# Turning the token tiles of five experts by VectorE in 32 by 32 blocks instead of by TensorE

## The chip, the cores and the metric

The kernel runs on one core of a Trainium2 chip. The metric is device time in microseconds (us). Before the change it is 337.43 us, the median of 3 runs from 336.81 to 337.83. A kernel drives five engines, each with its own queue in program order: TensorE (PE, matmuls and transposes; its weight loads are PEld), VectorE (DVE), ScalarE (ACT), GpSimd (POOL) and SyncE (SP). DMAs are issued from a queue of one of them and then run on 16 DMA engines.

## The reference

The program is an attention followed by a mixture of experts whose routing is a hash of the token's id. Cut to what matters:

```
q_n, k_n = rmsnorm(q, g_q), rmsnorm(k, g_k)          # 8 batches, 12 heads, 448 x 64
attn = softmax(q_n @ k_n^T / sqrt(64)) ; x = attn @ v  # as 3584 tokens x 768
expert = token_ids * 2654435761 % 8
for e in 0..7:
    xe = x[expert == e]                               # some 450 tokens
    out[expert == e] = max(xe @ w1[e], 0) @ w2[e]     # 768 x 1024, 1024 x 768
```

## The kernel before, in words

The first part (to about 160 us) is the attention. It writes x as 16-bit floats to a scratch tensor in HBM. The change does not touch it. The second part goes through the experts 0 to 7, one after the other; the stage of an expert is its two products.

Each expert has room for 480 tokens, in four row tiles: three of 128 tokens (kt 0 to 2) and one of 96 (kt 3). For each row tile, GpSimd issues an indirect DMA (`gather`, L230) that collects 128 rows of x from the scratch tensor into SBUF, tokens on the partitions. The tiles of two experts stand in a ring of eight places in the tile `kr` (`xg_ring`): the four places of expert e are used again by expert e+2. In the stage of expert e, `fetch(e + 2, ...)` (L1262) issues the four gathers of expert e+2.

The first product (`gemm1`, L1002) needs the tokens along the free dimension, so a row tile has to be turned: `turn` (L1055) calls `put_xT` (L238), which makes six TensorE transposes of 128 by 128 (L242) into a PSUM bank and one copy by VectorE (L244) into the tile `xT`. There are two buffers of xT. For the experts 2 to 6 these turns stand in front of the four column steps of the second product of the expert before (`before[e, kt]`, L1241 and L1272). The tiles of expert 1 are turned in the stage of expert 0, and those of expert 7 by four DMA transposes on SP's queue (L1065).

`gemm1` makes 48 matmuls of 480 columns: eight blocks of 128 rows of h, six matmuls each, in three PSUM buffers. After each block a ReLU brings it to `h_sb`, by ScalarE for the even blocks (L1011) and by VectorE for the odd ones (L1013). `gemm2` (L1018) goes over four column steps; each makes 16 matmuls (L1024) into one of two PSUM buffers `o_ps`, a copy to SBUF (`o_sb`, five buffers, L1034; ScalarE for steps 0 and 2, VectorE for 1 and 3), and an indirect DMA on GpSimd's queue that scatters the rows to the output (L1037).

Weights are loaded by GpSimd's queue too (L1090), three pieces of w1 and two of w2 an expert, converted from 32 to 16 bits on the way. The pieces of expert e+3 are issued in the stage of expert e, in the same queue as the scatters and the gathers. A DMA of this queue waits for the one eight places before it, since they share a semaphore. The order of the work is written out by hand: engines take their instructions in the order of the code.

Of the kernel before, what the change touches and what calls it, by code (L numbers as in the profile page):

```python
# [10 lines left out]
FP16 = mybir.dt.float16  # L11
# [9 lines left out]
def kernel(  # L21
# [12 lines left out]
    nc = tc.nc  # L34
# [3 lines left out]
    E = moe_w1.shape[0]  # L38
    F = moe_w1.shape[2]
    P = 128  # L40
    HP = H // 2
    CO = DIN // P
# [7 lines left out]
    CAP = 512  # L50
    FIT = 480
    LAST = FIT - 3 * P
    KT = CAP // P
# [31 lines left out]
    xg_ring = k_keep[:].rearrange("p (r d) -> p r d", d=DIN)  # L85
# [152 lines left out]
    def put_xT(xg, xT, col, bank, copy=None):  # L238
        xT_ps = bank.rearrange("p (c t) -> p c t", c=CO)
        n = LAST if col == KT - 1 else P  # L240
        for co in range(CO):
            nc.tensor.transpose(xT_ps[:, co, 0:n], xg[0:n, co * P:(co + 1) * P], ident16[0:n, 0:n])  # L242
        dst = xT[:, col] if xT is xT_e else xT[:, :, col * P:(col + 1) * P]
        (copy or nc.vector.tensor_copy)(dst[:, :, 0:n], xT_ps[:, :, 0:n])  # L244
# [719 lines left out]
    with tc.manual_schedule(), \  # L964
# [10 lines left out]
        def w1_view(e, w1_sb):  # L975
            return w1_sb[:].rearrange("p c (o f) -> p c o f" if e == 0 else "p c (f o) -> p c o f",
                                      o=FO)
# [13 lines left out]
        def gemm1(w1v, xT, h_sb, c0, c1, both=True, after=(), apart=0):  # L991
            banks = {}

            def products(fo, a0, a1):
                if fo not in banks:
                    banks[fo] = ps_h.tile([P, 512], FP32, name="h_ps")
                dst = banks[fo][:, a0 - c0:a1 - c0]
                if xT is xT_e:
                    dst = dst.rearrange("p (k t) -> p k t", t=P)
                for co in range(CO):  # L1000
                    src = xT[:, a0 // P:a1 // P, co, :] if xT is xT_e else xT[:, co, a0:a1]
                    nc.tensor.matmul(dst, lhsT=w1v[:, co, fo, :], rhs=src,  # L1002
                                     start=(co == 0), stop=(co == CO - 1))

            for fo in range(apart):
                products(fo, c0, c1 - P)
            for fo in range(FO):
                products(fo, c1 - P if fo < apart else c0, c1)
                h_ps = banks.pop(fo)
                if fo % 2 == 0 or not both:  # L1010
                    nc.scalar.activation(h_sb[:, fo, c0:c1], h_ps[:, :c1 - c0], AF.Relu)  # L1011
                else:
                    nc.vector.tensor_scalar(out=h_sb[:, fo, c0:c1], in0=h_ps[:, :c1 - c0],  # L1013
                                            scalar1=0.0, scalar2=None, op0=ALU.max)
                for f in after[fo] if after else ():
                    f()

        def gemm2(w2_sb, h_sb, col, idx, free=True, between=None, last=False):  # L1018
            w = LAST if free and col == KT - 1 else P
            o_ps = [ps_o.tile([P, DIN], FP32, name="o_ps")]  # L1020
            o_ps.append(ps_o.tile([P, DIN], FP32, name="o_ps") if last else o_ps[0])
            for d0, d1 in ((0, 512), (512, DIN)):
                for fo in range(FO):
                    nc.tensor.matmul(o_ps[d0 > 0][0:w, d0:d1], lhsT=h_sb[:, fo, col * P:col * P + w],  # L1024
                                     rhs=w2_sb[:, fo, d0:d1],
                                     start=(fo == 0), stop=(fo == FO - 1))
                if between and d0 == 0:
                    between()
                if last and d0 == 0:
                    o_sb = m_o.tile([P, DIN], FP32, name="o_sb")  # L1030
                    nc.scalar.copy(o_sb[0:w, 0:512], o_ps[0][0:w, 0:512])
            if not last:
                o_sb = m_o.tile([P, DIN], FP32, name="o_sb")
                (nc.vector.tensor_copy if col % 2 else nc.scalar.copy)(o_sb[0:w], o_ps[0][0:w])  # L1034
            else:
                nc.scalar.copy(o_sb[0:w, 512:DIN], o_ps[1][0:w, 512:DIN])
            scat = nc.gpsimd.indirect_dma_start(  # L1037
                out=out[:, :], out_offset=bass.IndirectOffsetOnAxis(ap=idx[0:w], axis=0),
                in_=o_sb[0:w], in_offset=None, bounds_check=N - 1, oob_is_err=False)
            if free:  # L1040

                tc.declare_no_dep(scat.ins, group="scatters", reason="disjoint rows")
                tc.add_to_no_dep_group("scatters", scat.ins)

        xgs = {c: xg_ring[:, c] for c in range(KT, 2 * KT - 1)}
        xTs = {0: xT_e}
# [8 lines left out]
        def turn(e, kt, copy=None):  # L1055
            if e not in xTs:
                xTs[e] = m_x.tile([P, CO, CAP], FP16, name="xT")
            bank = ps_x.tile([P, DIN], FP16, name="xT_ps")
            put_xT(xgs.pop(e * KT + kt), xTs[e], kt, bank[:], copy)

        def turn_by_dma(e):
            xTs[e] = m_x.tile([P, CO, CAP], FP16, name="xT")
# [173 lines left out]
        t = lambda e, kt: (lambda: turn(e, kt))  # L1236
        t0 = lambda e, kt: (lambda: turn(e, kt, nc.scalar.copy))
        before, between = {}, {}
        for e in range(1, E - 2):
            for kt in range(KT):  # L1240
                before[e, kt] = [t(e + 1, kt)]  # L1241
        before[0, 0], before[0, 1] = [t0(1, 0)], [t0(0, KT - 1)]
        between[0, 1] = t0(1, 1)
        before[0, 2] = [lambda: gemm1_late(w1_view(0, w_tiles[0][0]), xTs.pop(0), hs[0], EARLY, FIT)]
# [7 lines left out]
        for e in range(E):  # L1252
            w1_sb, w2_sb = w_tiles[e]
            h_sb = hs[e] = m_h.tile([P, FO, CAP], FP16, name="h_sb")
            after = [plan.get((e, "g", fo), []) for fo in range(FO)]
            if e == 0:
                gemm1(w1_view(e, w1_sb), xTs[e], h_sb, 0, EARLY, False, after, 2)
            else:
                if e == E - 2:
                    turn_by_dma(E - 1)  # L1260
                if e < E - 2:
                    fetch(e + 2, range(KT))  # L1262
                gemm1(w1_view(e, w1_sb), xTs.pop(e), h_sb, 0, FIT, True, after)
            if e:
                w_next(2)
            if e == 2:
                n_ov = nc.values_load(novi[0:1, 0:1], min_val=0, max_val=NOV)
            if e == E - 1:
                nc.gpsimd.drain()
            for kt in range(KT):  # L1270
                c = e * KT + kt
                for f in before.get((e, kt), []):  # L1272
                    f()
                gemm2(w2_sb, h_sb, kt, gidx[:, c:c + 1], between=between.get((e, kt)),
                      last=(c == E * KT - 1))
                for f in plan.get((e, "k", kt), []):
                    f()
                if e or kt > 1:
                    w_next(1)
            w_next(len(queue))  # L1280
            if e + 4 < E:
                queue += w_pieces(e + 4)
# [47 lines left out]
```

## Time and profile before

| what | value |
|---|---|
| median of 3 runs | 337.43 us (336.81 to 337.83) |
| the profiled execution | 337.81 us, span of the core 336.3 us |
| PE, DVE, ACT, POOL busy | 324.1, 197.6, 188.1, 149.4 us |
| first matmul of gemm1 of experts 1 to 7 | 182.80, 204.18, 225.57, 246.95, 268.34, 289.72, 309.84 us |
[...]

PE is busy for 96% of the span. The stages of experts 1 to 5, in which the next expert's tiles are turned by TensorE, take 21.38 us each; that of expert 6 takes 20.12 us. In the stages of experts 2 to 5 the DMA engines have no free time (a share over 1 means that packets overlap).

### The profile page before, as it was taken

To read this page: it belongs to the slowest core of one execution; us is meant where nothing else is said; L and a number is where in the kernel's file an instruction comes from. 1 tells how busy PE (TensorE), PEld (TensorE's weight loads), DVE (VectorE), ACT (ScalarE), POOL (GpSimd) and SP (SyncE) were. 2 spreads that over 40 slices of the span, in tenths; PEclk is the share of its full clock that TensorE was granted. 3 is DMA by queue.
4 is the path that set the end of the run, shared out by engine and by line. 5 is a ranking of instruction groups with operands and counts; after the bars stand their busy time and mean duration, and the time that the engine had idled before them with its cause. 6 is when DMAs were issued, how large, how long until landed. Compare 5 with 4: busy or idle time off the path is not lost. (4 is left out here: it accounts for less than half of the span.)

```text
span 336.3 us, 9185 instructions
## 1 busy us (share of the span) xinstructions
PE 324.1 (96%) x3885; PEld 226.0 (67%) x3885; DVE 197.6 (59%) x427; ACT 188.1 (56%) x287; POOL 149.4 (44%) x207
## 2 busy tenths in 40 slices
PE   7799999999999999998999999999999999999992
PEld 3567777777777776666677767677676676766751
DVE  4699999998989899984793343232323223222210
ACT  4699999999999999998443212202022021211211
POOL 8799925324340100003665853637557374303122
PEclk9999999999999999999999999999999999999998
DMA  6999999999999999332587899999999999923013
GB/s 132 201 201 204 211 231 197 242 200 237 203 244 211 248 225 238 69 84 72 154 167 215 167 209 246 263 274 250 258 263 255 271 244 255 281 47 133 25 51 117
DMA packets 45602, 65.54 MB, mean 195 GB/s; under 512 B 12727, under 2 KB 33423, under 8 KB 45432
## 3 DMA queue, kind: packets, MB, share of 16 engines
q0 software_dynamic: 39072, 58.32, 85.8%
q1 hardware_dynamic: 6328, 6.50, 7.2%
q8 instruction: 31, 0.51, 0.6%
q10 hardware_dynamic: 160, 0.11, 0.1%
q14 instruction: 11, 0.09, 0.1%
HBM read 89.29 MB, written 17.30 MB: 317 GB/s over the span
## 5 line engine op out<-in xcount | busy, mean ns | idle before, releaser
L660 ACT ACTIVATE expT<-sc_ps 128x896 bf16<-128x896 f32 x144 | 125.0, 959 | 2.5 <-PE sc_ps L637 2.2
L1024 PEld LDWEIGHTS <-h_sb 128*128 128x128 f16 (+1 forms) x512 | 51.2, 104 | 30.3 <-ACT h_sb L1011 0.4
L1024 PE MATMUL o_ps<-w_sb,h_sb 128*128 128x512 f16 (+3 forms) x384 | 66.3, 326 | 0.0
L1037 POOL DMA_INDIRECT out_dram<-o_sb,gidx x32 | 35.0, 1095 | 62.4 <-ACT o_sb L1034 29.6
L1011 ACT ACTIVATE h_sb<-h_ps 128x480 f16<-128x480 f32 (+1 forms) x36 | 19.9, 553 | 68.4 <-PE h_ps L1002 64.4
L230 POOL DMA_INDIRECT kr<-x_scratch,gidx x32 | 32.7, 1021 | 50.6 <-DVE qT L629 36.6
L1002 PEld LDWEIGHTS <-w_sb 128*128 128x128 f16 x300 | 39.7, 135 | 16.0 <-issue 0.3
L1002 PE MATMUL h_ps<-xT,w_sb 128*128 128x480 f16 x240 | 49.4, 366 | 0.0
L1013 DVE TENSOR_SCALAR h_sb<-h_ps 128x480 f16<-128x480 f32 x28 | 18.4, 658 | 47.2 <-PE h_ps L1002 42.2
L1034 ACT COPY o_sb<-o_ps 128x768 f32<-128x768 f32 x16 | 12.8, 799 | 59.3 <-PE o_ps L1024 47.0
L637 PE MATMUL sc_ps<-qT,kT 64*128 64x448 f16 x288 | 44.3, 356 | 0.8 <-DVE qT L629 0.4
L678 PEld LDWEIGHTS <-expT 128*128 128x128 bf16 x846 | 36.8, 97 | 9.5 <-DVE x_sb L738 4.6
L678 PE MATMUL av_ps<-v,expT 128*128 128x65 bf16 x828 | 41.5, 193 | 0.3 <-DVE x_sb L738 0.2
L1034 DVE COPY o_sb<-o_ps 128x768 f32<-128x768 f32 (+1 forms) x15 | 14.3, 956 | 37.6 <-PE o_ps L1024 32.9
L306 POOL DMA_DIRECT2D vr<-in_v_dram x36 | 23.8, 673 | 18.3 <-DMA kr<-in_k_dram 10.4
L738 DVE TENSOR_TENSOR x_sb<-av_ps,srec 128x448 f16<-128x448 f32 x47 | 29.3, 623 | 1.3
L663 ACT ACTIVATE expT<-sc_ps 128x448 bf16<-128x448 f32 x48 | 28.6, 598 | 0.1
L387 PEld LDWEIGHTS <-ident 128*128 128x128 f16 x576 | 22.7, 97 | 7.9 <-issue 2.8
L683 PE MATMUL av_ps<-v,expT 128*128 128x130 bf16 x138 | 24.0, 220 | 0.0
L1024 PE MATMUL o_ps<-kr,h_sb 128*128 128x512 f16 (+3 forms) x128 | 21.6, 326 | 0.0
L244 DVE COPY xT<-xT_ps 128x768 f16<-128x768 f16 (+1 forms) x21 | 11.0, 524 | 17.9 <-PE xT_ps L242 15.8
L1002 PE MATMUL h_ps<-xT,qr 128*128 128x480 f16 x96 | 19.8, 366 | 0.0
(225 smaller groups left out, 441.8 us busy)
## 6 DMA issues: line engine op xcount, KB each, us to landing
w_sb<-in_moe_w_dram POOLq DMA_DIRECT2D x18, 512.0 KB
w_sb<-in_moe_w_dram POOLq DMA_DIRECT2D x8, 768.0 KB
kr<-in_k_dram POOLq DMA_DIRECT2D x7, 672.0 KB
qr<-in_q_dram POOLq DMA_DIRECT2D x7, 672.0 KB
x_scratch<-x_sb SPq DMA_DIRECT2D x15, 288.0 KB, 6.9
w_sb<-in_moe_w_dram POOLq DMA_DIRECT2D x2, 1536.0 KB
qr<-in_moe_w_dram POOLq DMA_DIRECT2D x6, 512.0 KB
vr<-in_v_dram POOLq DMA_DIRECT2D x14, 192.0 KB
```

The costliest lines, as they stand in the source:

```text
L230: nc.gpsimd.indirect_dma_start(out=xg[0:idx.shape[0], :], out_offset=None, in_=x_dram[0:rows, :], in_offset=bass.IndirectOffsetOnAxis(ap=i ...
L306: eng.dma_start(out=dst[64 * half:64 * half + 64, :, s0:s0 + cnt, :].rearrange("p n s d -> p n (s d)"), in_=runs(t, h0 + HP * hh, 1, n, to ...
L637: nc.tensor.matmul(sc[:, hh, :S], lhsT=kT[64 * hh:64 * hh + 64, P * j:P * j + P], rhs=qT[64 * hh:64 * hh + 64, :], start=True, stop=True)
L660: nc.scalar.activation(expT[:, 2 * j:2 * j + 2, :], sc[:, :, :S], AF.Exp, bias=0.0, scale=1.0)
L663: nc.scalar.activation(expT[:, 6, :], sc[:, 0, :S], AF.Exp, bias=0.0, scale=1.0)
L678: nc.tensor.matmul(av[:, 2 * t + hh, :], lhsT=expT[:, tl(hh, j), P * t:P * t + P], rhs=v8[:, i, vs(hh, j), 0:D + 1], start=(hh == 0 and t ...
L683: nc.tensor.matmul(av[:, 2 * t:2 * t + 2, :], lhsT=expT[:, 6, P * t:P * t + P], rhs=v8[:, i, 0::7, 0:D + 1], start=False, stop=False)
L738: nc.vector.tensor_tensor(out=xs[b][:, :, hp * D:hp * D + D], in0=av[:, :, :D], in1=srec[:, :, None].to_broadcast([P, SL, D]), op=ALU.mult)
L1002: nc.tensor.matmul(dst, lhsT=w1v[:, co, fo, :], rhs=src, start=(co == 0), stop=(co == CO - 1))
L1024: nc.tensor.matmul(o_ps[d0 > 0][0:w, d0:d1], lhsT=h_sb[:, fo, col * P:col * P + w], rhs=w2_sb[:, fo, d0:d1], start=(fo == 0), stop=(fo == ...
L1034: (nc.vector.tensor_copy if col % 2 else nc.scalar.copy)(o_sb[0:w], o_ps[0][0:w])
L1037: scat = nc.gpsimd.indirect_dma_start(out=out[:, :], out_offset=bass.IndirectOffsetOnAxis(ap=idx[0:w], axis=0), in_=o_sb[0:w], in_offset=N ...
```

## The change

A new function `turn_blocks(e)` turns the four row tiles of an expert with 16 VectorE instructions, SBUF to SBUF. Each of them takes 32 partitions (32 tokens of each of the four tiles) and writes 32 other partitions; within an instruction each block of 32 by 32 is turned. 12 of them handle four tiles, 4 of them (the last 32 tokens) three tiles, since the fourth has 96 tokens. It is called for the experts 2 to 6, at the start of the stage of the expert before, behind the gathers of the expert after. The 24 TensorE transposes and four VectorE copies for each of these experts go. In the stages of experts 1 to 5 all eight ReLUs and all four output copies are ScalarE's; in the stages of experts 0, 6 and 7 they are shared as before.

```
--- before.py
+++ after.py
@@ -1015,7 +1015,7 @@
                 for f in after[fo] if after else ():
                     f()
 
-        def gemm2(w2_sb, h_sb, col, idx, free=True, between=None, last=False):
+        def gemm2(w2_sb, h_sb, col, idx, free=True, between=None, last=False, by_v=True):
             w = LAST if free and col == KT - 1 else P
             o_ps = [ps_o.tile([P, DIN], FP32, name="o_ps")]
             o_ps.append(ps_o.tile([P, DIN], FP32, name="o_ps") if last else o_ps[0])
@@ -1031,7 +1031,7 @@
                     nc.scalar.copy(o_sb[0:w, 0:512], o_ps[0][0:w, 0:512])
             if not last:
                 o_sb = m_o.tile([P, DIN], FP32, name="o_sb")
-                (nc.vector.tensor_copy if col % 2 else nc.scalar.copy)(o_sb[0:w], o_ps[0][0:w])
+                (nc.vector.tensor_copy if by_v and col % 2 else nc.scalar.copy)(o_sb[0:w], o_ps[0][0:w])
             else:
                 nc.scalar.copy(o_sb[0:w, 512:DIN], o_ps[1][0:w, 512:DIN])
             scat = nc.gpsimd.indirect_dma_start(
@@ -1057,6 +1057,21 @@
                 xTs[e] = m_x.tile([P, CO, CAP], FP16, name="xT")
             bank = ps_x.tile([P, DIN], FP16, name="xT_ps")
             put_xT(xgs.pop(e * KT + kt), xTs[e], kt, bank[:], copy)
+
+        def turn_blocks(e):
+            xT = xTs[e] = m_x.tile([P, CO, CAP], FP16, name="xT")
+            c0 = e * KT % (2 * KT)
+            xg = xg_ring[:, c0:c0 + KT].rearrange("p k (c m r) -> p k m c r", m=4, r=32)
+            dst = xT[:].rearrange("p c (g r) -> p c g r", r=32)
+            for kt in range(KT):
+                xgs.pop(e * KT + kt)
+            for i in range(4):
+                n = KT if 32 * i < LAST else KT - 1
+                g = slice(i, i + 4 * (n - 1) + 1, 4)
+                for m in range(4):
+                    nc.vector.transpose(
+                        out=dst[32 * m:32 * m + 32, :, g].rearrange("p c k r -> p k c r"),
+                        in_=xg[32 * i:32 * i + 32, 0:n, m])
 
         def turn_by_dma(e):
             xTs[e] = m_x.tile([P, CO, CAP], FP16, name="xT")
@@ -1236,9 +1251,6 @@
         t = lambda e, kt: (lambda: turn(e, kt))
         t0 = lambda e, kt: (lambda: turn(e, kt, nc.scalar.copy))
         before, between = {}, {}
-        for e in range(1, E - 2):
-            for kt in range(KT):
-                before[e, kt] = [t(e + 1, kt)]
         before[0, 0], before[0, 1] = [t0(1, 0)], [t0(0, KT - 1)]
         between[0, 1] = t0(1, 1)
         before[0, 2] = [lambda: gemm1_late(w1_view(0, w_tiles[0][0]), xTs.pop(0), hs[0], EARLY, FIT)]
@@ -1260,7 +1272,8 @@
                     turn_by_dma(E - 1)
                 if e < E - 2:
                     fetch(e + 2, range(KT))
-                gemm1(w1_view(e, w1_sb), xTs.pop(e), h_sb, 0, FIT, True, after)
+                    turn_blocks(e + 1)
+                gemm1(w1_view(e, w1_sb), xTs.pop(e), h_sb, 0, FIT, e >= E - 2, after)
             if e:
                 w_next(2)
             if e == 2:
@@ -1272,7 +1285,7 @@
                 for f in before.get((e, kt), []):
                     f()
                 gemm2(w2_sb, h_sb, kt, gidx[:, c:c + 1], between=between.get((e, kt)),
-                      last=(c == E * KT - 1))
+                      last=(c == E * KT - 1), by_v=e in (0, E - 2, E - 1))
                 for f in plan.get((e, "k", kt), []):
                     f()
                 if e or kt > 1:
```

On VectorE, this is what stands before in the stage of one expert of 2 to 5: four ReLUs (`h_sb<-h_ps`), four copies of turned tiles and two output copies.

```order
L1013 TENSOR_SCALAR h_sb<-h_ps 128x480 x4
L244 COPY xT<-xT_ps 128x6x128 x2
L1034 COPY o_sb<-o_ps 128x768
L244 COPY xT<-xT_ps 128x6x128
L244 COPY xT<-xT_ps 128x6x96
L1034 COPY o_sb<-o_ps 96x768
```

And this is what stands there now, in the stages of expert 2 and, from the last row on, of expert 3 (`kr_69` holds the ring of gathered tiles; the names in brackets are the semaphores waited for, DMASW those of GpSimd's DMAs).

```order
L1072 STREAM_TRANSPOSE xT<-kr_69 32x4x6x32 [waits DMASW5_49,DMASW6_49,DMASW0_49,DMASW7_49,PE_49,Activation_49]
L1072 STREAM_TRANSPOSE xT<-kr_69 32x4x6x32 x11
L1072 STREAM_TRANSPOSE xT<-kr_69 32x3x6x32 x4
L1280 TENSOR_LOAD novi [waits DVE_49]
L1072 STREAM_TRANSPOSE xT<-kr_69 32x4x6x32 [waits DMASW4_49,DMASW3_49,DMASW5_49,DMASW2_49,PE_49]
```

VectorE's stage now holds nothing but the 16 transposes, and the first of them waits for all four gathers of the expert to be turned.

On ScalarE, before, for the stages of experts 1 and 2 and the start of 3 (`h_sb` is a ReLU, `o_sb` an output copy):

```order
L1011 ACTIVATE h_sb<-h_ps 128x480 x4
L1034 COPY o_sb<-o_ps 128x768 x2
L1011 ACTIVATE h_sb<-h_ps 128x480 x4
L1267 TENSOR_LOAD novi
L1034 COPY o_sb<-o_ps 128x768 x2
```

And now, for the same stages:

```order
L1011 ACTIVATE h_sb<-h_ps 128x480 x8
L1034 COPY o_sb<-o_ps 128x768 x3
L1034 COPY o_sb<-o_ps 96x768
L1011 ACTIVATE h_sb<-h_ps 128x480 x8
L1280 TENSOR_LOAD novi
```

ScalarE has eight ReLUs and four copies in a stage where it had four and two. On TensorE the 24 weight loads and transposes of L242 are gone from each of the five stages, and on GpSimd the order is unchanged, but the first gather of an expert now waits for VectorE where it waited for TensorE.

## Rows read from the trace of the kernel before

**Rows 1.** Windows by stage: length, busy us (instructions) of PE, PEld, DVE, ACT, POOL, PEclk, DMA, GB/s.

```profile
182.80:204.18 21.38, 21.38 (x138) 14.68 (x137) 7.42 (x13) 3.88 (x6) 13.00 (x16) 1.00 0.91 186
204.18:225.57 21.39, 21.39 (x139) 14.70 (x138) 6.56 (x10) 3.88 (x6) 11.56 (x13) 1.00 1.06 262
...
268.34:289.72 21.38, 21.38 (x138) 14.69 (x137) 6.49 (x10) 3.88 (x6) 12.51 (x14) 1.00 1.03 266
289.72:309.84 20.12, 20.12 (x114) 13.44 (x113) 4.54 (x6) 3.88 (x6) 3.89 (x4) 1.00 0.47 109
```

**Rows 2.** Timeline of TensorE, experts 2 and 6: start, us, engine, line.

```profile
204.18 9.88 PE L1002 MATMUL h_ps<-xT,qr 128*128 128x480 f16 x48
213.90 0.50 PE L242 MATMUL xT_ps<-ident,kr 128*128 128x128 f16 x6
214.24 2.76 PE L1024 MATMUL o_ps<-kr,h_sb 128*128 128x512 f16 x16
...
289.72 9.88 PE L1002 MATMUL h_ps<-xT,qr 128*128 128x480 f16 x48
299.44 10.56 PE L1024 MATMUL o_ps<-kr,h_sb 128*128 128x512 f16 x64
```

**Rows 3.** Timeline of GpSimd: start, us, engine, line [idle before it, and its releaser].

```profile
185.74 0.96 POOL L230 DMA_INDIRECT kr<-x_scratch,gidx  x1 [0.30 <-issue]
...
191.73 1.08 POOL L230 DMA_INDIRECT kr<-x_scratch,gidx  x1 [0.30 <-issue]
...
208.64 1.07 POOL L1037 DMA_INDIRECT out_dram<-o_sb,gidx  x1 [0.50 <-DMA kr<-x_scratch,gidx]
...
211.60 0.58 POOL L1090 DMA_DIRECT2D w_sb<-in_moe_w_dram  x1
...
227.43 1.08 POOL L1037 DMA_INDIRECT out_dram<-o_sb,gidx  x1 [3.42 <-DMA w_sb<-in_moe_w_dram]
...
234.99 1.08 POOL L230 DMA_INDIRECT kr<-x_scratch,gidx  x1 [0.62 <-issue]
...
247.65 1.07 POOL L1037 DMA_INDIRECT out_dram<-o_sb,gidx  x1 [3.42 <-DMA w_sb<-in_moe_w_dram]
...
267.80 1.07 POOL L1037 DMA_INDIRECT out_dram<-o_sb,gidx  x1 [3.46 <-DMA kr<-in_moe_w_dram]
...
279.86 0.98 POOL L230 DMA_INDIRECT kr<-x_scratch,gidx  x1 [0.34 <-issue]
```

**Rows 4.** Timeline of SP's queue: the transposes of expert 7's tiles.

```profile
288.92 6.88 SPq L1065 DMA_TRANSPOSE xT<-kr  x4
```

**Rows 5.** DMAs that write the tile xT: the time from issue to landing.

```profile
DMA to landing us min/median/max: 2.8/4.3/4.8
```

**Rows 6.** Windows (as Rows 1) around the gathers of expert 2.

```profile
186.00:188.00 2.00, 2.00 (x11) 1.43 (x10) 0.23 (x2) 0.57 (x1) 1.69 (x3) 1.00 0.55 149
188.00:190.00 2.00, 2.00 (x12) 1.41 (x11) 0.52 (x1) 0.57 (x1) 2.00 (x3) 1.00 0.80 99
```

**Rows 7.** VectorE by form: out<-in, xcount | busy us, mean ns | idle before.

```profile
L244 DVE COPY xT<-xT_ps 128x768 f16<-128x768 f16 x15 | 8.3, 551 | 9.7 <-PE xT_ps L242 7.6 <-PE o_ps L1024 2.1
L1034 DVE COPY o_sb<-o_ps 128x768 f32<-128x768 f32 x8 | 7.7, 958 | 20.7 <-PE o_ps L1024 18.2 <-PE xT_ps L242 2.4
...
L1172 DVE TENSOR_REDUCE slot_f<-rank 128x28 f32<-128x224 f32 x1 | 0.6, 566 | 0.0
```

**Rows 8.** Timeline of VectorE: two instructions back to back.

```profile
193.29 0.55 DVE L244 COPY xT<-xT_ps 128x768 f16<-128x768 f16 x1
193.76 0.41 DVE L1219 TENSOR_TENSOR ovc<-iota_f,oend 128x256 f32<-128x256 f32 x1
```

**Rows 9.** ScalarE by form from 160 us on (columns as Rows 7).

```profile
L1011 ACT ACTIVATE h_sb<-h_ps 128x480 f16<-128x480 f32 x28 | 16.0, 571 | 62.4 <-PE h_ps L1002 60.6 <-issue 1.9
L1034 ACT COPY o_sb<-o_ps 128x768 f32<-128x768 f32 x16 | 12.8, 799 | 59.3 <-PE o_ps L1024 47.0 <-issue 7.2 <-DMA out_dram<-o_sb,gidx 5.1
```

**Rows 10.** Timeline of all engines at 172 us (columns as Rows 3).

```profile
172.00 1.78 DVE L1188 TENSOR_TENSOR hi<-iota_h,hl 128x1568 f16<-128x1568 f16 x1
172.33 2.38 POOL L1037 DMA_INDIRECT out_dram<-o_sb,gidx  x1 [1.92 <-ACT o_sb L1034]
```

More of the change, by code (lines that the diff above doesn't have):

```diff
@@ L1016, in gemm1, with gemm2 @@
                     f()
-        def gemm2(w2_sb, h_sb, col, idx, free=True, between=None, last=False):
+        def gemm2(w2_sb, h_sb, col, idx, free=True, between=None, last=False, by_v=True):
             w = LAST if free and col == KT - 1 else P
@@ L1033, in gemm2 @@
                 o_sb = m_o.tile([P, DIN], FP32, name="o_sb")
-                (nc.vector.tensor_copy if col % 2 else nc.scalar.copy)(o_sb[0:w], o_ps[0][0:w])
+                (nc.vector.tensor_copy if by_v and col % 2 else nc.scalar.copy)(o_sb[0:w], o_ps[0][0:w])
             else:
@@ L1059, in turn, with turn_blocks @@
             put_xT(xgs.pop(e * KT + kt), xTs[e], kt, bank[:], copy)
+        def turn_blocks(e):
+            xT = xTs[e] = m_x.tile([P, CO, CAP], FP16, name="xT")
+            c0 = e * KT % (2 * KT)
+            xg = xg_ring[:, c0:c0 + KT].rearrange("p k (c m r) -> p k m c r", m=4, r=32)
+            dst = xT[:].rearrange("p c (g r) -> p c g r", r=32)
+            for kt in range(KT):
+                xgs.pop(e * KT + kt)
+            for i in range(4):
+                n = KT if 32 * i < LAST else KT - 1
+                g = slice(i, i + 4 * (n - 1) + 1, 4)
+                for m in range(4):
+                    nc.vector.transpose(
+                        out=dst[32 * m:32 * m + 32, :, g].rearrange("p c k r -> p k c r"),
+                        in_=xg[32 * i:32 * i + 32, 0:n, m])
         def turn_by_dma(e):
@@ L1238 @@
         before, between = {}, {}
-        for e in range(1, E - 2):
-            for kt in range(KT):
-                before[e, kt] = [t(e + 1, kt)]
         before[0, 0], before[0, 1] = [t0(1, 0)], [t0(0, KT - 1)]
@@ L1262 @@
                     fetch(e + 2, range(KT))
-                gemm1(w1_view(e, w1_sb), xTs.pop(e), h_sb, 0, FIT, True, after)
+                    turn_blocks(e + 1)
+                gemm1(w1_view(e, w1_sb), xTs.pop(e), h_sb, 0, FIT, e >= E - 2, after)
             if e:
@@ L1274 @@
                 gemm2(w2_sb, h_sb, kt, gidx[:, c:c + 1], between=between.get((e, kt)),
-                      last=(c == E * KT - 1))
+                      last=(c == E * KT - 1), by_v=e in (0, E - 2, E - 1))
                 for f in plan.get((e, "k", kt), []):
```

## The prediction

> **What bounds the kernel now.** I read the windows by stage first. In the five stages in which tiles are turned, TensorE is busy for all of the 21.38 us, at a granted clock of 1.00; the stage of expert 6, which holds no turn of TensorE's, takes 20.12 us, also without a gap [rows 1]. So TensorE sets the time, and 24 transposes cost 1.26 us of a stage. The timeline shows them in the path: the first column step of gemm2 starts behind six of them at 214.24, while in the stage of expert 6 it follows gemm1 at once [rows 2]. The same windows show the second limit: the DMA engines have no free time in the stages of experts 2 to 5, and move some 262 to 267 GB/s [rows 1].
>
> GpSimd's timeline shows what this does to a gather. The first gather of expert 3 is seen by a waiting scatter at about 208.3, while the four were issued from 191.7 on: it stood behind weights. SP's first transpose of expert 7 waits for that expert's first gather until 288.9 [rows 3, 4]. Four experts in 80.6 us is 20.15 us an expert, and the waits for weights, which end at 227.43, 247.65 and 267.80, have the same step of 20.2 [rows 3]. The DMA queue thus keeps a pace of its own, faster than TensorE's 21.38 and equal to its 20.12. The gathers come some 17 us ahead of their use, which is enough while TensorE turns tiles late in a stage. It is the number to look at when the turning takes most of a stage.
>
> **The change part by part.** *Removed from TensorE:* 5 stages by 21.38 - 20.12 = 1.26 us, 6.3 us in all [rows 1]. This is the most that can be had, since nothing else on TensorE changes.
>
> *Added on VectorE:* 16 instructions for each expert, 12 of 4 x 6 x 32 = 768 elements a partition and 4 of 576. No row shows this operation. The nearest are copies of 768 elements: 551 ns at two elements a step (16-bit), 958 ns at one (32-bit). Their difference gives 1.06 ns an element at the slower rate and 0.14 us that is fixed [rows 7]. At one element a step 576 elements take 0.76 us, and the 16 take 12 x 0.958 + 4 x 0.76 = 14.5 us, which I call B. The low end is the 16-bit copy's rate: 12 x 0.551 + 4 x 0.45 = 8.4 us. The high end is the slowest row per element, a reduction over a strided view, 566 ns for 224 elements or 1.88 ns an element [rows 7]: 1.59 and 1.23 us, B = 24.0. I take 14.5, the row whose shape and kind (a plain move) is nearest, at the rate of the operation that cannot pair elements.
>
> Whether B is a plain sum of durations is a second question. Two neighbours overlap by 0.08 us in the one place shown (0.55 us at 193.29, the next at 193.76) [rows 8]. 16 times that would make B 13.2. Each of the 16 writes other partitions than the one before, which no row shows; I take no overlap, and keep 13.2 for the range. [...]
>
> *Where it lies:* the 16 wait for all four gathers of the expert, and gemm1 of that expert needs all 16, since each matmul takes all partitions and tokens. So gemm1 of expert e cannot start before L(e) + B + 0.2, where L is the landing of the last gather and 0.2 an estimated allowance for the two handovers (GpSimd's rows show 0.30 between two of its instructions). Nor before the stage in front of it plus 20.12.
>
> L: a gather moves 128 x 768 x 2 bytes = 0.197 MB, 0.75 us at 262 GB/s; the last three (one of 96 rows) come 2.05 us behind the first. From 208.3 in steps of 20.15: L(3) = 210.35, L(4) = 230.5, L(5) = 250.65, L(6) = 270.8. The bound above for L(3) is 211.3, where GpSimd issued without a wait the DMA that stands eight behind that gather [rows 3]. Expert 2's gathers find the DMA engines 0.55 to 0.80 busy [rows 6]; the last one's issue ends at 186.7 [rows 3], and with the shortest time to landing that the view of xT has, 2.8 us [rows 5], L(2) = 189.5.
>
> Starts of gemm1: expert 2: 189.5 + 14.7 = 204.2 (TensorE could at 182.80 + 20.12 = 202.9). Expert 3: the later of 224.3 and 225.05. Expert 4: 245.2 by both. Expert 5: 265.35. Expert 6: 285.5, against 289.72 now [rows 2]. The gain at these starts is 0, 0.5, 1.75, 3.0 and 4.2 us: the turns give TensorE 1.26 us a stage, and the wait for VectorE takes back 2.1 of the 6.3. Expert 7's tiles are done by 288.92 + 6.88 = 295.8 [rows 4], ten us ahead of gemm1 at 305.6, so that everything from expert 6 on moves by the same 4.2.
>
> *Moved to ScalarE:* four more ReLUs of 0.571 and two more copies of 0.799 a stage [rows 9], 3.88 us more, 7.8 of 20.1 in all. One ReLU has to fit into the 9.88 / 8 = 1.24 us of a block of gemm1, a copy into 2.6 us of a column step [rows 2]. Cost nothing; the cover is gone only if a copy stands still, since the next expert's ReLUs are queued behind it. A copy waits for the scatter five before. Those of expert 5 come up to 4.2 us earlier; the second scatter of expert 4 had landed by 279.6, since a gather that waits for it was issued at 279.86 [rows 3], and the copy that takes its buffer would come at some 282.8. Three us of slack remain, and three buffers of gemm1 lie behind it.
>
> *Waits on GpSimd:* the gathers of expert e+2 now wait for the 16 transposes of expert e, done before gemm1 of e. The gathers of expert 5 were issued at 234.99 [rows 3], ten us behind the 225 at which expert 3's transposes end. Nothing.
>
> *Sum:* the profiled execution took 337.81 us; less 4.2 it is 333.6. It is the slowest of the runs shown, 0.38 above their median of 337.43, to which the forecast refers: 333.2. With B of 13.2 to 15.8 (0.08 less or more an instruction) or L a us later, 331.9 to 335.5.
>
> **The rivals.** *The full gain:* if B is at most 12.4, from the 16-bit copy's rate or overlap with gathers that land together, no expert waits and all 6.3 us are had: 331.1. For it: 8.4 is in the bounds, and expert 3's stage needs only a little. Against: it wants over 2 us off a sum that rests on the plain rate.
>
> *Slower, since VectorE becomes the pace:* at B = 18.9 the gain is gone (289.72 - 270.8). Above 20.15 the next expert's 16 queue behind the last ones, and each of the five costs the excess: gemm1 of expert 6 starts at 189.7 + 5 B. At the 24.0 of the strided reduction this is 309.7, 20 us late: 357.4; at B = 21, 342.4. For it: blocks of 32 strewn over source and target, an operation that no row times. Against: B must be 30% over the plain rate even to cost the gain.
>
> *GpSimd slowed by VectorE:* a scatter's issue took 2.38 us while VectorE ran an operation with two SBUF inputs, against 0.96 to 1.08 elsewhere [rows 3, 10]. If the transposes do the same to all eight indirect DMAs of a stage, GpSimd's 11.56 us [rows 1] grow by 11 to 22.6, over the 20.15, and the gathers fall behind by 2.4 us in each of three to four stages: L(6) about 279.3, 4.3 us slower than now after B, 341.7. Against: the transposes have one input, and beside one-input copies the issues kept their 1.0. [...]
>
> *Little or nothing:* the last gather of some expert lands 3 to 5 us later than I put it. Any one of the five suffices, since the bounds lie within half a us of each other. Then 335.5 to 337.4.
>
> **How the numbers follow.** Forecast, TensorE held back by the transposes: 0.50. Full gain: 0.24. Little or nothing: 0.14, of which 0.04 is within 0.3% (1.0 us, about what a measurement of this kernel can tell from no change). VectorE as the pace: 0.08. GpSimd slowed: 0.04. So faster by over 0.3%: 0.84; within: 0.04; slower: 0.12. The range leaves out the slower cases and the very edge of the full gain: 330.8 to 336.9.
>
> **What would show it.** In the profile after, the transposes should last 0.96 and 0.76 us, 14.5 us from the first start to the last end, the first of expert 6 waiting for a gather until about 271. TensorE should have gaps in front of gemm1 of experts 2 to 6, about 1.3 us at the first, 0.7 at the second and near none at the others, and a stage should hold 20.12 us of matmuls. ScalarE's waits should be for TensorE alone. The prediction is wrong if TensorE has no gaps (full gain), if transposes stand back to back from one expert to the next (VectorE is the pace), if GpSimd's issues last over 2 us, or if expert 6's first transpose starts past 273.

## The result and the profile after

The changed kernel takes 333.0 us (median of 4 runs, 332.68 to 334.84) against 337.5 us before (336.81 to 337.83); the ratio is 0.9874, 95% interval 0.9845 to 0.9903. The forecast was 333.2, in a range of 330.8 to 336.9. The profiled execution took 332.74 us, its span is 331.1 us.

TensorE's timeline after, the first product of the experts 1 to 7 and, in brackets, its idle time and what ended it:

```profile
182.94 9.88 PE L1002 MATMUL h_ps<-xT,w_sb 128*128 128x480 f16 x48
192.66 10.56 PE L1024 MATMUL o_ps<-w_sb,h_sb 128*128 128x512 f16 x64
203.75 9.88 PE L1002 MATMUL h_ps<-xT,qr 128*128 128x480 f16 x48 [0.52 <-DVE xT L1072]
...
224.37 9.88 PE L1002 MATMUL h_ps<-xT,w_sb 128*128 128x480 f16 x48 [0.34 <-DVE xT L1072]
...
244.55 9.88 PE L1002 MATMUL h_ps<-xT,w_sb 128*128 128x480 f16 x48
...
264.72 9.88 PE L1002 MATMUL h_ps<-xT,w_sb 128*128 128x480 f16 x48
...
284.86 9.88 PE L1002 MATMUL h_ps<-xT,qr 128*128 128x480 f16 x48
...
304.98 9.88 PE L1002 MATMUL h_ps<-xT,w_sb 128*128 128x480 f16 x48
```

The second product now follows the first at once, as it did only in the stage of expert 6 [rows 2]. gemm1 of expert 6 starts 101.92 us behind that of expert 1, where it was 106.92 (289.72 - 182.80). Five stages of 20.12 would be 100.60; the 1.32 us more are the gaps in front of experts 2 and 3 and less than 0.1 at each of the other three.

VectorE's timeline after (start, length of the 16, idle before and its releaser) shows what TensorE waited for:

```profile
188.78 14.92 DVE L1072 STREAM_TRANSPOSE xT<-kr 32x768 f16<-32x768 f16 x16 [4.68 <-DMA kr<-x_scratch,gidx]
...
209.41 14.91 DVE L1072 STREAM_TRANSPOSE xT<-kr 32x768 f16<-32x768 f16 x16 [4.30 <-ACT h_sb L1011]
229.58 14.92 DVE L1072 STREAM_TRANSPOSE xT<-kr 32x768 f16<-32x768 f16 x16 [5.26 <-DMA kr<-x_scratch,gidx]
249.75 14.92 DVE L1072 STREAM_TRANSPOSE xT<-kr 32x768 f16<-32x768 f16 x16 [5.25 <-PE h_ps L1002]
269.89 14.92 DVE L1072 STREAM_TRANSPOSE xT<-kr 32x768 f16<-32x768 f16 x16 [5.22 <-DMA kr<-x_scratch,gidx]
```

188.78 + 14.92 = 203.70, and gemm1 of expert 2 starts at 203.75. The same holds for the other four, to within 0.05 us. Two rows name ScalarE or TensorE as releaser; the first transpose waits for several semaphores, and the one that came last by the profile is put down. In both cases it was the gather: by the trace the last one landed at 209.23 and 249.53, 0.2 us before the transposes began. The starts from expert 3 on have a step of 20.14 to 20.17 us, the pace that the prediction read from the DMA queue.

The trace also shows what a gather waits for. All DMAs of GpSimd's queue whose landing it holds landed in the order in which they were issued. The last gather of expert 2 landed 2.8 us after the start of its issue. The four of expert 3 were issued from 191.87 to 195.88, right behind four pieces of weights; the last of these pieces landed at 206.86, the gathers between 207.75 and 209.23.

The groups of VectorE's instructions, from 182 to 290 us, give the duration that no row of before had (columns as [rows 7]):

```profile
L1072 DVE STREAM_TRANSPOSE xT<-kr 32x768 f16<-32x768 f16 x60 | 58.1, 969 | 25.4 <-DMA kr<-x_scratch,gidx 15.2 <-PE h_ps L1002 5.2 <-ACT h_sb L1011 4.3
L1072 DVE STREAM_TRANSPOSE xT<-kr 32x576 f16<-32x576 f16 x20 | 15.4, 772 | 0.3
```

969 and 772 ns are 1.03 ns an element and 0.18 us fixed. ScalarE's two groups, the ReLUs and the output copies, wait for TensorE alone (rows of the whole execution):

```profile
L1011 ACT ACTIVATE h_sb<-h_ps 128x480 f16<-128x480 f32 (+1 forms) x56 | 31.3, 560 | 48.6 <-PE h_ps L1002 48.6
...
L1034 ACT COPY o_sb<-o_ps 128x768 f32<-128x768 f32 (+1 forms) x26 | 20.8, 799 | 54.5 <-PE o_ps L1024 54.5
```

And the windows by stage (columns as [rows 1]):

```profile
182.94:203.75 20.81, 20.29 (x115) 13.45 (x113) 15.70 (x18) 7.41 (x12) 12.99 (x16) 1.00 0.92 184
203.75:224.37 20.62, 20.28 (x112) 13.46 (x112) 16.00 (x19) 7.58 (x13) 11.61 (x13) 1.00 1.07 257
...
264.72:284.86 20.14, 20.14 (x115) 13.47 (x112) 14.72 (x16) 7.76 (x12) 11.27 (x13) 1.00 1.06 255
```

VectorE's work in a stage grew from 6.5 to 14.7 us and ScalarE's from 3.9 to 7.8 [rows 1]; a stage of TensorE is its 20.1 us of matmuls plus the gap in front, and the DMA engines are as full as before (a share of 0.92 to 1.07, where it was 0.91 to 1.07).

### The profile page after: what moved, and what is told of

Same layout as the page of the kernel before. It is cut to its first block, busy times and chain, and to the rows that moved or that the text cites. A ratio compares the mean times of both kernels' runs of the same rounds, so it can differ in the third digit from the quotient of the medians.

```text
span 331.1 us, 8985 instructions
## 1 busy us (share of the span) xinstructions
PE 318.2 (96%) x3765; PEld 219.7 (66%) x3765; DVE 239.3 (72%) x457; ACT 207.5 (63%) x317; POOL 149.5 (45%) x207
## 5 line engine op out<-in xcount | busy, mean ns | idle before, releaser
L1072 DVE STREAM_TRANSPOSE xT<-kr 32x768 f16<-32x768 f16 (+1 forms) x80 | 73.6, 920 | 25.7 <-DMA kr<-x_scratch,gidx 15.2
L1024 PEld LDWEIGHTS <-h_sb 128*128 128x128 f16 (+1 forms) x512 | 52.2, 104 | 31.3
L1024 PE MATMUL o_ps<-w_sb,h_sb 128*128 128x512 f16 (+3 forms) x384 | 64.2, 326 | 0.0
L1011 ACT ACTIVATE h_sb<-h_ps 128x480 f16<-128x480 f32 (+1 forms) x56 | 31.3, 560 | 48.6 <-PE h_ps L1002 48.6
L1034 ACT COPY o_sb<-o_ps 128x768 f32<-128x768 f32 (+1 forms) x26 | 20.8, 799 | 54.5 <-PE o_ps L1024 54.5
L230 POOL DMA_INDIRECT kr<-x_scratch,gidx x32 | 32.6, 1020 | 49.3 <-DVE qT L629 37.1
L637 PEld LDWEIGHTS <-kT 64*128 64x128 f16 x288 | 12.3, 93 | 9.5 <-issue 2.2
L1105 POOL DMA_DIRECT2D w_sb<-in_moe_w_dram x20 | 13.7, 692 | 9.4 <-DMA w_sb<-in_moe_w_dram 6.8
```

Source lines behind the costliest of these rows:

```text
L230: nc.gpsimd.indirect_dma_start(out=xg[0:idx.shape[0], :], out_offset=None, in_=x_dram[0:rows, :], in_offset=bass.IndirectOffsetOnAxis(ap=i ...
L637: nc.tensor.matmul(sc[:, hh, :S], lhsT=kT[64 * hh:64 * hh + 64, P * j:P * j + P], rhs=qT[64 * hh:64 * hh + 64, :], start=True, stop=True)
L1072: nc.vector.transpose(out=dst[32 * m:32 * m + 32, :, g].rearrange("p c k r -> p k c r"), in_=xg[32 * i:32 * i + 32, 0:n, m])
```

## The experiments

Theory A is the prediction's: gemm1 of an expert starts when its last gather has landed and the 16 transposes behind it (the chain) have ended, or when TensorE is ready, whichever is later; the landing goes by the DMA queue. Theory B: the chain does not bind, and 1.3 us are missed for another reason. The phase ahead ends up to 1.2 us earlier or later from one execution to the next (gemm1 of expert 1 starts between 181.66 and 184.03 in the profiles), so beside the time each run has the distance from gemm1 of expert 1 to that of expert 6. Each ratio is to the kernel before as measured beside that run (medians of 337.34 to 337.50).

| run | what differs from the changed kernel | time, us (median; range) | ratio to before (95%) | distance, us |
|---|---|---|---|---|
| before | | 337.43 (336.59 to 339.61) | 1 | 106.92 |
| changed, again | nothing | 332.29 (331.66 to 333.76) | 0.9857 (0.9826 to 0.9887) | 101.98 |
| e1 | 12 transposes instead of 16 | 330.80 (330.28 to 332.47) | 0.9796 (0.9769 to 0.9824) | 100.59 |
| e2 | 20 for experts 3 to 6 | 338.19 (336.59 to 341.54) | 1.0016 (0.9988 to 1.0043) | 108.05 |
| e3 | gathers earlier in the queue | 334.49 (333.64 to 338.14) | 0.9942 (0.9905 to 0.9979) | 102.67 |
| e4 | e3, short transposes first | 335.71 (333.71 to 337.25) | 0.9936 (0.9906 to 0.9966) | 104.70 |
| e5 | short transposes first alone | 332.91 (331.94 to 334.22) | 0.9864 (0.9833 to 0.9895) | 102.33 |
| e6 | e4, seven output buffers | 332.09 (331.11 to 332.64) | 0.9845 (0.9809 to 0.9881) | 100.60 |
| e7 | no transposes on VectorE | 337.36 (336.70 to 338.87) | 0.9997 (0.9979 to 1.0015) | 106.92 |
| e9 | e6, expert 7's gathers at their old place | 331.08 (330.38 to 331.82) | 0.9804 (0.9778 to 0.9831) | 100.60 |
| e10 | e9, 20 transposes for experts 3 to 6 | 330.78 (330.25 to 330.95) | 0.9800 (0.9773 to 0.9827) | 100.60 |
| e11 | ReLUs and copies shared again | 393.67 (one run) | | 163.12 |
| e12 | 32 half transposes | 334.35 (one run) | | 104.06 |

**The chain made shorter (e1).**

```
-            for i in range(4):
+            for i in range(3):
...
+        nc.scalar.copy(...)   # the last 32 tokens of three tiles, unturned, behind the ReLUs
```

> This kernel leaves out the turning of the last 32 tokens of the first three tiles of experts 2 to 6 (ScalarE copies them unturned, behind the ReLUs), so VectorE's chain for an expert is 12 transposes, some 11.8 us instead of 14.9. Theory A (gemm1 of an expert starts when its last gather has landed and the chain after it has ended): the gaps of 0.69 and 0.5 us in front of experts 2 and 3 and the 0.13 us after them go, TensorE is without gaps, and 1.3 us are gained: 333.0 becomes 331.7. Theory B (the chain does not bind, the gain of 6.3 is missed for another reason, such as slower matmuls beside the transposes): unchanged, 333.0.

The gaps are gone: TensorE's five stages are 20.12 us each, a distance of 100.59, and the time is lower by 1.5 to 2.2 us (330.80; 332.29 and 333.0 with the gaps), where 1.3 were expected. From gemm1 of expert 1 to the end the profiled executions took 148.44 against 149.80 us, 1.36 less; the medians also hold the phase ahead, which the edit does not touch. VectorE's row for expert 6 is now

```profile
271.23 11.78 DVE L1072 STREAM_TRANSPOSE xT<-kr 32x768 f16<-32x768 f16 x12 [8.15 <-DMA kr<-x_scratch,gidx]
```

which ends at 283.0, 1.6 us ahead of gemm1 at 284.62. Theory B falls.

**The chain made longer (e2).**

```
-            for i in range(4):
+            for i in ((0, 1, 2, 3, 3) if e > 2 else range(4)):
```

> The last four transposes of each of experts 3 to 6 are made twice, so their chain is 3.1 us longer (18.0); expert 2's is as it was. Theory A: the landings of the gathers have the same step as TensorE's stages, so every expert from 3 on is late by the same 3.1 us, and it is paid once, less the slack that there is none of: gemm1 of expert 3 at 227.4 instead of 224.4, and then stages of 20.1; time 336.1. Theory B: VectorE has five idle us in a stage and takes the 3.1 there: 333.0. Theory C (each expert's wait is paid anew): 4 x 3.1, 345.

The wait was paid once, in front of expert 3, as theory A has it, and not anew for each expert (theory C). But the time is 338.2, not 336.1 (336.59 to 341.54; the profiled execution took 339.85). TensorE's timeline in e2:

```profile
228.52 12.81 PE L1002 MATMUL h_ps<-xT,w_sb 128*128 128x480 f16 x48 [3.57 <-DVE xT L1072]
...
251.57 9.88 PE L1002 MATMUL h_ps<-xT,w_sb 128*128 128x480 f16 x48
```

The gap is the 0.34 of the changed kernel and 3.2. Behind it the same 48 matmuls take 12.81 us instead of 9.88. The windows around it show the granted clock of those matmuls (the last three columns are granted clock, DMA share and GB/s):

```profile
224.90:228.50 3.60, 0.06 (x1) 0.00 (x0) 3.44 (x5) 0.79 (x1) 0.26 (x2) 0.88 1.01 315
228.50:232.00 3.50, 3.48 (x9) 1.49 (x9) 1.36 (x2) 0.57 (x1) 3.20 (x4) 0.50 1.11 222
232.00:235.00 3.00, 3.00 (x10) 1.40 (x9) 2.96 (x4) 0.57 (x1) 2.39 (x4) 0.59 1.10 266
235.00:238.00 3.00, 3.00 (x17) 2.13 (x16) 2.96 (x4) 1.42 (x3) 1.90 (x3) 1.00 1.13 281
```

Behind a gap of 3.57 us the granted clock was 0.50 until some 234: nine matmuls ran in 3.5 us, where some 17 do at 1.00 (48 in 9.88 us). The wait of 3.2 us thus cost 6.1 in this execution; by the medians the kernel lost 5.2 to 5.9. The expectation missed this.

**The landing made earlier (e3, e4).**

```
-                    fetch(e + 2, range(KT))          # at the start of the stage of expert e
...
+                if kt == 1 and 1 <= e < E - 3:       # behind the second column step
+                    fetch(e + 3, range(KT))
+                if e == 0 and kt == 3:
+                    fetch(3, range(KT))
...
-            for i in range(4):                       # e4 only
+            for i in (3, 0, 1, 2):
```

> Only the place of the gathers in GpSimd's queue is changed: those of expert 3 stand right behind those of expert 2, those of 4 to 7 two column steps earlier, in front of two pieces of w2 and two scatters. Theory A with the landing set by what stands ahead in the DMA queue: gathers of expert 3 land at about 193 instead of 209, those of 4 to 6 some 8 us earlier; the gap in front of expert 3 (0.5) and the small ones after it go, the one in front of expert 2 stays: 332.4, and the transposes of experts 4 to 6 no longer wait for a gather. If the landing were set by GpSimd's issue alone, the gathers would move by the some 5 us by which they are issued earlier.

> As the run with early gathers, and the four transposes that need only the first three tiles (the last 32 tokens of each) stand first of the 16, so VectorE begins when the third gather has landed, 1.3 us before the fourth for expert 2. Theory A: the gap of 0.69 us in front of expert 2 closes as well, TensorE has no gap from expert 1 to the end, and all of the 6.3 us are had: 331.7 (1.3 under 333.0). Theory B: 333.0.

The landing moved, by less than said: in e3 expert 4's transposes start 39.98 us behind gemm1 of expert 1 (46.64 in the changed kernel), which is 6.7 us earlier where some 8 were expected by the queue and some 5 by the issue alone. Expert 3's start without any wait for a gather; those of experts 4 to 6 still wait for one, against the expectation. By the trace the last gather of expert 4 was issued 6.6 us earlier and landed 6.7 earlier, that of expert 5 5.0 and 6.6 (both counted from gemm1 of expert 1). So e3 does not separate the place in the queue from the time of the issue. In e4 the gap in front of expert 2 is closed (202.99 - 182.87 = 20.12). But both kernels are slower than the changed one, by 1.5 and 2.7 us (medians). TensorE stands still at a new place, in the middle of the first products of experts 3 and 6, and ScalarE in front of it; e4's rows of TensorE and ScalarE:

```profile
229.17 7.92 PE L1002 MATMUL h_ps<-xT,w_sb 128*128 128x480 f16 x30 [2.25 <-ACT h_sb L1011]
...
292.44 6.24 PE L1002 MATMUL h_ps<-xT,qr 128*128 128x480 f16 x30 [1.06 <-ACT h_sb L1011]
```

```profile
221.50 0.80 ACT L1034 COPY o_sb<-o_ps 128x768 f32<-128x768 f32 x1 [2.55 <-DMA out_dram<-o_sb,gidx]
227.85 0.79 ACT L1034 COPY o_sb<-o_ps 96x768 f32<-96x768 f32 x1 [5.55 <-DMA out_dram<-o_sb,gidx]
228.55 1.49 ACT L1011 ACTIVATE h_sb<-h_ps 128x480 f16<-128x480 f32 x3
```

The last copy of expert 2 waits until 227.85 for a scatter; three ReLUs of expert 3 stand behind it in ScalarE's queue and run one after the other once it is through. All three buffers of gemm1 are full by then (18 matmuls are three blocks of six). The gathers went ahead of scatters, and these now free the output buffers too late. Behind the gap of 2.25 us the granted clock is again down to 0.50, and the 30 matmuls take 7.92 us (6.24 behind the gap of 1.06); e4's windows, columns as [rows 1]:

```profile
229.17:231.00 1.83, 1.83 (x7) 0.97 (x7) 1.80 (x3) 0.87 (x2) 0.85 (x1) 0.67 1.11 222
231.00:233.00 2.00, 2.00 (x7) 0.84 (x6) 1.97 (x3) 0.57 (x1) 1.06 (x2) 0.50 1.12 217
```

**Short transposes first alone (e5).**

```
-            for i in range(4):
+            for i in (3, 0, 1, 2):
```

> The changed kernel with one difference: the four transposes that need only the first three tiles stand first of the 16. The gathers keep their places. Theory A (gemm1 waits for the last landing plus the chain behind it): VectorE begins 1.3 us earlier for expert 2 and about 0.6 us earlier for the others, the gaps of 0.69 and 0.5 us close, and no scatter is moved, so no copy waits; gemm1 of expert 6 starts 100.6 us (5 x 20.12) behind that of expert 1 instead of 101.9; time 331.7. Theory B (the gaps do not come from the chain): 101.9 as before, 333.0.

Half a miss. The gap in front of expert 2 closes (203.25 - 183.13 = 20.12), but the time does not fall, 332.91 against 332.29 of the changed kernel beside it. The gaps come back further on: 0.43 and 0.56 us in front of experts 3 and 4 and 0.22 in front of 6. The one in front of expert 3 follows from theory A, and the expectation's sum missed it. With the first gap closed TensorE is ready 0.69 us earlier, and expert 3's transposes began only 0.61 us earlier (25.86 us behind gemm1 of expert 1 instead of 26.47). To close every gap, the later chains had to end 1.2 to 1.3 us earlier, not 0.6. Expert 4's transposes start 46.71 us behind gemm1 of expert 1, although they wait for one gather less; it was 46.64 and 46.62 in the two profiles of the changed kernel, and 47.0 in e1. By the trace the third gather landed only 0.33 us ahead of the fourth (229.71 and 230.04), and the four landed 0.3 to 0.6 us later than in the changed kernel. So the landings vary by some tenths from one execution to the next, in a chain where any one of five sets the end.

**Seven output buffers (e6).**

```
-         tc.tile_pool(name="m_o", bufs=5) as m_o, \
+         tc.tile_pool(name="m_o", bufs=7) as m_o, \
```

> The run with early gathers and the short transposes first, now with seven output buffers instead of five. In that run TensorE stood still twice, 2.3 and 1.1 us, behind ScalarE, whose fourth copy of a stage waited for a buffer. If that wait is for the scatter five copies before, which the gathers have pushed back in the DMA queue, seven buffers take it away: no gap, gemm1 of expert 6 100.6 us behind that of expert 1 (104.7 then), 331.7. If ScalarE is late for another reason, such as too many ReLUs and copies in its queue, the gaps stay and the time is 334 to 336.

The distance is 100.60: no gap is left among experts 1 to 6, and the wait for scatters was the cause in e3 and e4. The time, 332.09, is hardly under the 332.29 (the ranges overlap; from gemm1 of expert 1 to the end the profiled executions took 149.14 and 149.83 us), since a gap opened elsewhere, in front of expert 7:

```profile
303.35 9.91 PE L1002 MATMUL h_ps<-xT,w_sb 128*128 128x480 f16 x48 [0.49 <-DMA xT<-kr]
```

```profile
283.13 16.91 SPq L1080 DMA_TRANSPOSE xT<-kr  x4
```

The early gathers let SP issue the DMA transposes of expert 7's tiles at 283.13, while the last weights were still on their way (by the trace they landed at 289.3 and 294.5). The four took 16.9 us of SP's queue instead of 6.1 (at 289.04 in the changed kernel), and the last landed at 303.2.

**The move to ScalarE alone (e7) and the changed kernel again (e8).** The edit of e7 is the change without `turn_blocks`: TensorE turns as before.

> One part alone: the kernel before with only the move of ReLUs and output copies to ScalarE in the stages of experts 1 to 5; the tiles are turned by TensorE and copied by VectorE as before. If the move is free, as the prediction costed it, stages stay at 21.38 us and the time at 337.4. If it had a price (ScalarE in the path of the column steps) or a gain of its own, it would show in the stage: 21.6 or more would be 338.5.

> The changed kernel once more, beside the others on the same chip: 333.0, gemm1 of expert 6 101.9 us behind that of expert 1, with gaps in front of experts 2 and 3 alone.

e7 is the same as before (0.9997), with the same distance of 106.92: the move costs nothing and brings nothing by itself. The changed kernel repeats: 332.29, distance 101.98, gaps in front of experts 2 (0.66 over the 20.12), 3 (0.55) and, not expected, 5 (0.17).

**The version without gaps (e9), and the long chain in it (e10).**

```
-                if kt == 1 and 1 <= e < E - 3:       # of e6
+                if kt == 1 and 1 <= e < E - 4:
...
+                if e == E - 3:
+                    fetch(E - 1, range(KT))
```

> As the run with early gathers and seven output buffers, but the gathers of expert 7 stand where they stood before. There they were early as well, SP's four DMA transposes of expert 7's tiles then ran beside the last weights and took 16.9 us, and gemm1 of expert 7 waited 0.5 us for them. Expected: those transposes begin at about 288 again and take 6 to 7 us; no gap from expert 1 to the end, gemm1 of expert 7 120.7 us (6 x 20.12) behind that of expert 1; 331.5. If the wait for the DMA transposes had nothing to do with the gathers' place, it stays, and so does 332.1.

> The kernel of the run above with the short transposes of experts 3 to 6 made twice, 3.3 us more for each, as in the run that added them to the changed kernel (where gemm1 of expert 6 came 6.1 us later, 3.2 of it a gap and 2.9 a stage at a lower clock). Theory A: with the gathers landing 7 us earlier a chain of 18.2 us has ended before TensorE is ready, so nothing is lost: 331.5 to 332, no gap. If a longer chain costs time by itself (VectorE's accesses beside TensorE's or GpSimd's), 334 or more.

e9 is the fastest version that turns every tile whole and once: 331.08 us, 6.4 under the 337.5 beside it. Its profile has TensorE without a gap from the start of expert 1's gemm1 to that of expert 7's, 120.72 us or 6 x 20.12:

```profile
182.75 9.88 PE L1002 MATMUL h_ps<-xT,w_sb 128*128 128x480 f16 x48
...
303.47 9.88 PE L1002 MATMUL h_ps<-xT,w_sb 128*128 128x480 f16 x48
```

SP's transposes start at 290.68 and take 6.87 us. By the ratios to before it is at 0.9804 (to 0.9831) against 0.9874 (from 0.9845) and 0.9857 (from 0.9826) for the changed kernel. In e10 the chain of expert 6 is 18.2 us long and still ends ahead of gemm1 at 282.28:

```profile
263.35 18.20 DVE L1072 STREAM_TRANSPOSE xT<-kr 32x576 f16<-32x576 f16 x20 [1.80 <-DMA kr<-x_scratch,gidx]
```

The added transposes, which cost 6.1 us in e2, cost nothing here. Nor does VectorE's longer work lengthen TensorE's: its 48 matmuls of gemm1 take 9.88 us beside the transposes, as before.

**The transposes without the move (e11).**

```
-                gemm1(..., h_sb, 0, FIT, e >= E - 2, after)
+                gemm1(..., h_sb, 0, FIT, True, after)
...
-                      last=(c == E * KT - 1), by_v=e in (0, E - 2, E - 1))
+                      last=(c == E * KT - 1), by_v=True)
```

> The other part alone: the transposes by VectorE, but ReLUs and output copies shared by ScalarE and VectorE as before. VectorE's ReLUs and copies of a stage stand behind the 16 transposes of the next expert in its queue, so the second block of gemm1 is not brought out before the transposes have ended; with three buffers TensorE stops at the fifth block. A stage is then the 14.9 us of transposes, and behind them the rest of gemm1 (some 6 us) and gemm2 (10.5): 31 to 33 us instead of 20.1 in five stages, 390 us. If VectorE's queue did not matter: 333.

393.67 us in one run, as expected to 1%; the stage of expert 1 took 36.5 us, the other four 31.1 to 32.6. In the stage of expert 1 VectorE's first three ReLUs come when the transposes of expert 2 have ended, and TensorE has stood still for 13.19 us by then:

```profile
188.53 14.91 DVE L1072 STREAM_TRANSPOSE xT<-kr 32x768 f16<-32x768 f16 x16 [4.66 <-DMA kr<-x_scratch,gidx]
203.47 1.79 DVE L1013 TENSOR_SCALAR h_sb<-h_ps 128x480 f16<-128x480 f32 x3
```

```profile
204.19 4.82 PE L1002 MATMUL h_ps<-xT,w_sb 128*128 128x480 f16 x12 [13.19 <-DVE h_sb L1013]
```

With the 16 transposes in one block of VectorE's queue, the move to ScalarE, free by itself, is what makes them pay. An order in which VectorE's ReLUs and copies stand between the transposes was not tried.

**Half transposes (e12).**

```
+                    for c in (slice(0, 3), slice(3, 6)):
...
-                        out=dst[32 * m:32 * m + 32, :, g]..., in_=xg[32 * i:32 * i + 32, 0:n, m])
+                        out=dst[32 * m:32 * m + 32, c, g]..., in_=xg[32 * i:32 * i + 32, 0:n, m, c])
```

> Each transpose is cut in two (three of the six column groups each), so that the second half reads and writes the same partitions as the first, and only every other instruction writes other partitions than the one before it. It measures the step from start to start. If instructions that write other partitions are kept apart and those that write the same ones overlap by some 0.08 us, a pair takes about 2 x 0.55 less 0.08 and the 32 take 16.1 us; if no transposes overlap, 32 x 0.55 (less for the short ones), 16.9 or more. Either way the chain is 1.2 to 2.5 us longer than 14.9, and the time 334.5 to 336, more if a gap of TensorE lowers its clock.

The first two of e12 (same partitions) and, below, the first two of the changed kernel (other target partitions), each pair merged by the timeline:

```profile
188.38 1.02 DVE L1073 STREAM_TRANSPOSE xT<-kr 32x384 f16<-32x384 f16 x2 [4.77 <-DMA kr<-x_scratch,gidx]
```

```profile
188.78 1.95 DVE L1072 STREAM_TRANSPOSE xT<-kr 32x768 f16<-32x768 f16 x2 [4.68 <-DMA kr<-x_scratch,gidx]
```

A half lasts 0.547 us by its group, so two that write the same partitions overlap by 0.07 us (2 x 0.547 - 1.02); two of 0.969 that write others lie 0.01 us apart. The trace has the same within all 32 of e12: 0.06 to 0.07 us of overlap where the partitions are the same, 0.01 us of distance where they change. The chain is 15.88 us, 0.96 longer than in the changed kernel, and the time 334.35; both lie a little under what was expected (1.2 longer, 334.5). The distance, 104.06, grew by 2.1 us, more than the chain: by the trace the last gathers of experts 3, 4 and 5 landed 0.5, 1.2 and 1.6 us later in this execution than in the changed kernel's. Why they did is not shown.

## Why the prediction was right

*The size and its source.* 4.2 us were forecast for the profiled execution; it gained 5.07 (337.81 - 332.74), 4.86 of it at the start of expert 6. The starts of experts 2 to 6 were forecast at 204.2, 225.05, 245.2, 265.35 and 285.5 and came at 203.75, 224.37, 244.55, 264.72 and 284.86. The mechanism held step by step: the five starts are the ends of the five chains, and lengthening or shortening a chain, or moving the gathers, moved or closed the gaps (e1, e2, e9, e10).

*The chain B.* 14.5 forecast, 14.92 measured: 969 and 772 ns an instruction instead of 958 and 760, and 0.01 us between two. Two more copies of before, columns as [rows 7] and [rows 8], show the two rates between which the forecast chose, and which it calls two elements a step and one:

```profile
L244 DVE COPY xT<-xT_ps 128x576 f16<-128x576 f16 x6 | 2.7, 456 | 8.2 <-PE xT_ps L242 8.2
```

```profile
162.30 0.16 DVE L1127 COPY et<-h_ps 128x16 f32<-128x16 f32 x1
```

Beside the 551 and 958 ns for 768 elements [rows 7], 456 ns for 576 give 0.49 ns an element for the 16-bit copies, and 0.16 us for 16 give 1.06 for the 32-bit ones. That the transposes, of 16-bit elements, would run at the second was the author's estimate; they took 1.03, so the row of the plain 32-bit copy was the right one to take. Taking no overlap was right as well, though it was the author's choice and no row of before showed it: in e12 two transposes that read and write the same 32 partitions overlap by 0.07 us, and two that write others lie 0.01 us apart.

*The landings L.* Forecast 189.5, 210.35, 230.5 and 250.65 for experts 2 to 5; by the trace the last gathers landed at 188.65, 209.23, 229.46 and 249.53. The forecast was 0.85 us too late for the first and 1.0 to 1.1 for the others, so the pace of the queue was right and its offset was not. For expert 2 the 2.8 us to landing count from the start of an issue (2.77 here), and the sum counted them from its end. For the others, the four gathers landed within 1.4 to 1.5 us where the sum had 2.05, and the first of expert 3 at 207.75 instead of 208.3. The two handovers, from landing to VectorE and from VectorE to TensorE, came to 0.17 to 0.27 us; 0.2 was allowed. L was too late and B too short, so the starts, 0.45 to 0.7 us too late, came out nearer than L: in part luck.

*Two readings that cost nothing.* The stage of expert 4 moved 258 GB/s, less than the 262 to 267 named for experts 2 to 5. The 295.8 us at which expert 7's tiles were said to be done is the end of SP's instructions; by the trace before, the last landed at 297.3, still eight us ahead of its use.

*The gaps.* 1.3 and 0.7 us forecast in front of experts 2 and 3, 0.69 and 0.50 measured, as L for expert 2 was late by more than B was short.

*ScalarE.* Costed at nothing, and e7 shows nothing. The cover named for it, the landing of scatters, is real: where it was taken away, ScalarE waited 4.83 (e3) and 5.55 us (e4) for a scatter, and TensorE stood still behind it for 0.78 and 2.25 us.

*The rivals.* The full gain needed a chain of at most 12.4 us; the changed kernel's takes 14.92, and e1 (11.8) and e9 show what the full gain is worth (330.8 and 331.1; 331.1 was named). VectorE did not become the pace, since 14.92 us is well under the 20.15 of a stage. GpSimd's issues of gathers and scatters stayed at 0.97 to 1.08 us beside the transposes. No gather came late enough to take the gain away, though e2 shows how near that was: with chains 3.3 us longer there was none, as 3.2 us went to the gap and 2.9 to the matmuls behind it, at a granted clock of 0.50.

## What to carry to other kernels

Work that is taken off the busiest engine and given to an idle one needs a bound of its own: when its input lands, how long it takes, and when its result is used. Here landing and length together ended up to 1.3 us behind the use: a longer chain cost its whole excess and more (3.2 us of gap and 2.9 behind it in e2), and a shorter one (e1) or an earlier landing with more output buffers (e9) gave the rest of the gain. The changed kernel had 4.9 of the 6.3 us. In the full queue here the gathers that were moved ahead pushed other transfers back: look for who waits for those (the scatters that free output buffers: a copy waited 5.55 us for one in e4) and for what the earlier landing sets off (DMA transposes that started beside weights: 16.9 us of SP's queue in e6 instead of 6.1) before counting the gain.

## What the runs showed of the hardware that had not been expected

A wait of TensorE of 3.57 us cost 2.9 us more behind it, one of 2.25 us cost 1.7 us more (30 matmuls in 7.92 us instead of 6.24); in both the granted clock was down to 0.50 after the gap (e2, e4). Behind gaps of 0.52 and 0.34 us in the changed kernel and of 0.78 and 1.32 in e3 it stayed at 1.00; behind those of 0.24 to 1.22 us in e12 the 48 matmuls took their 9.88 us. The same four DMA transposes took 6.1 us of SP's queue in the changed kernel, where they began behind the weights, and 16.9 us in e6, beside the last of them. In the changed kernel a gather of expert 2 landed 2.8 to 3.2 us after the start of its issue, with the DMA engines 0.52 to 0.85 busy, and those of experts 3 to 5 landed 10 to 16 us after it, in a queue full of weights.
